# First loads cut finer, the checks' counts spread over the last batch, and the last store ahead of the verdict

## The chip, the cores and the metric

The kernel runs on one core of a Trainium2 chip. The metric is the device time of one execution in microseconds (us). The time before is a median of 313.62 us over 14 runs, which lie between 312.78 and 316.0.

A core has a matrix engine (PE, TensorE), a vector engine (DVE, VectorE), an engine for functions of one element (ACT, ScalarE), a general engine (POOL, GpSimd) and one that issues transfers (SP, SyncE). Each works through a queue of its own in order; they wait for one another on semaphores. Sixteen DMA engines move the data.

## The reference

Attention with inducing points, followed by a gated feed-forward layer:

```python
B, N, m, C = (4, 12480, 32, 128)
def mab(q, kv):
    s = scale * (q @ kv.transpose(0, 2, 1))
    s = s - s.max(-1, keepdims=True)
    a = np.exp(s)
    a /= a.sum(-1, keepdims=True) + 1e-09
    return a @ kv
h = mab(I, x)             # 32 rows for each batch
y = mab(x, h)             # 12480 rows for each batch
u = y @ w_in              # 128 -> 2048
g = u * np.clip(u + 3.0, 0.0, 6.0) / 6.0
out = g @ w_out           # 2048 -> 128
```

All inputs and the output are float32. Input and output are 25.6 MB each.

## The kernel before

**What it computes.** For each of the four batches it makes `h` (32 rows) in a first pass over x. As long as `u` stays under 3 in size, the second layer is `u*u/6 + u/2` times w_out, and the output for a row of x is a quadratic form in its 32 attention weights. The kernel builds small coefficient matrices for this from `h` and the weights (`c_...` functions), and the second pass over x (`b_...` functions) needs only them.

**The conditions.** That form is right only if some conditions hold: the largest `u` of the 32 rows is at most 3 (`g_all`), the sums of the first softmax lie between 1e-20 and 1e30 (`d_all`), and the second softmax's numbers are not too small (`r_all`, `nf_all`). The kernel keeps these values in four tables for all batches. After the last chunk it counts on DVE how many of the entries satisfy each condition (lines 922 to 939, five counts, each with an accumulator that goes to one column of `cnt`), adds the counts over the partitions with a matmul (L941), adds the five sums (L943), and compares the total with the number of entries (L945). The result `bad_i` is read by all five engines into a register (L949); if it isn't zero, `direct_path` computes everything again without the form (L952). With this input it is zero.

**How the work is cut.** The 12480 rows of a batch are six groups of 128 x 16 rows and a rest of 48 x 4. A group has four chunks of 128 x 4 rows, the rest is one chunk: 25 chunks for a batch, 100 in all.

**First pass, first batch** (`a_first`, L340): x is loaded in DMAs on GpSimd's queue, `load_x` (L110). In program order: both halves of group 0 (L125), then, after the identity is made, the rest, groups 1, 2 and 3 whole, and groups 4 and 5 in halves (L165), all ahead of the weights (L160, L161). The work goes by half groups: cast to bf16 (L359), transpose on PE (L369, copied by L371), weights of the softmax (L378, exponential L385), and the weighted sum (L392). A cast of a first half is split between ACT and DVE, a second half's is ACT's.

**Between the passes of the first batch** (`c_first`, L627): ACT casts the weights, PE adds up the denominators (`c_den`, L456), DVE inverts them (L473), PE transposes the sums (`c_HT`, L479), DVE scales them to `HT` (L482), and from this the coefficients are built (L488 to L603). Matmuls on zeros (`warm`, L176) keep PE busy: two ahead of all this, two between `c_den` and `c_HT`, one behind `c_HT`.

**Main loop** (L873): step t finishes chunk t and prepares chunk t + 2, and between PE's matmuls it fills in the first pass and the coefficients of the next batch; in the last batch (t from 75 on) there is nothing to fill in. On DVE a step is: the evacuation of chunk t - 1 (`b_evac`, L833, PSUM times r to `os`), the product of chunk t + 1 (L793, which needs the transfer `d`, L764), sometimes nf (L720), and the reciprocal of chunk t + 1 (L738). On PE it is: the linear part (`b_lin`, L801, into one of two PSUM banks of `op`, which the evacuation frees), 16 matmuls of the quadratic part (`b_quad`, L817) and the features of chunk t + 2 (L777). When a group is complete its 1 MB goes out by one DMA (L842), in the last batch on SP's queue, whose other DMAs are those of `d`.

**The end**: chunk 99 is the last rest of 48 x 4 rows. Its evacuation and store (96 KB) are called at L946, behind the counts and the verdict.

Of the kernel before, what the change touches and what calls it, by code (L numbers as in the profile page):

```python
# [9 lines left out]
FP32 = mybir.dt.float32  # L10
# [4 lines left out]
ALU = mybir.AluOpType  # L15
AX = mybir.AxisListType
# [8 lines left out]
TG = 16  # L25
SL = 4
XBUF = 5
# [13 lines left out]
def kernel(  # L41
# [8 lines left out]
    nc = tc.nc  # L50
    P = nc.NUM_PARTITIONS
    B, N, C = x.shape
    M = inducing.shape[0]
# [15 lines left out]
    NGR = len(groups)  # L69
# [11 lines left out]
    with ExitStack() as es:  # L81
# [25 lines left out]

        xs, xbs = {}, {}

        def load_x(b, g, parts=1):  # L110
            t0, p, n = groups[g]
            src = x[b, t0 : t0 + p * n, :].rearrange("(p i) c -> p i c", i=n)
            if n < TG:
                t = xlast.tile([P, n, C], FP32R, name="xl")
            elif b == 0 and g == XBUF:

                t = osp.tile([P, TG, C], FP32R, name="x5", tag="os")
            else:
                t = xin.tile([P, TG, C], FP32R, name="xr")
            for h in range(parts):  # L120
                lo, hi = h * n // parts, (h + 1) * n // parts
                nc.gpsimd.dma_start(t[:p, lo:hi, :], src[:, lo:hi, :])
            xs[(b, g)] = t

        load_x(0, 0, 2)  # L125

        held = []
        NF = NGR - 1 if rest else NGR
# [34 lines left out]

        make_identity(nc, ident[:, :])
        for g in (NF, *range(1, XBUF + 1)):  # L165
            load_x(0, g, 2 if g in (XBUF - 1, XBUF) else 1)
        wake = const.tile([P, 512], BF16, name="wake")
        nc.vector.memset(wake[:, :], 0.0)
        ident_b = const.tile([P, P], BF16, name="ident_b")
# [2 lines left out]
        def warm(n):  # L172

            wp = psF.tile([P, 512], FP32, name="wp", tag="fb")
            for _ in range(n):
                nc.tensor.matmul(wp[:, :], lhsT=wake[:, :P], rhs=wake[:, :])  # L176
# [67 lines left out]
        def a_begin(b):  # L244
            S[b] = {
                "xT": xTp.tile([P, N], BF16, name="xT"),
                "hnd": psH.tile([P, 512], FP32, name="hnd", tag="hnd"),
                "dacc": cst.tile([P, TG * M], FP32, name="dacc"),
            }
# [377 lines left out]
        def c_first():  # L627

            warm(2)
            nc.scalar.copy(w_in_b[:, : F // 2], w_in_r[:, : F // 2].bitcast(FP32))  # L630
            c_den(0)
            nc.scalar.copy(w_in_b[:, F // 2 :], w_in_r[:, F // 2 :].bitcast(FP32))
            warm(2)
            c_HT(0)
            warm(1)

            def cast_w(i, j):
                nc.scalar.copy(w_out_b[:, i:j, :], w_out_r[:, i:j, :].bitcast(FP32))

            cast_w(0, 4)  # L640
            c_G(0, 0, 6)
            sq = lambda *jbs: [c_sq(0, jb) for jb in jbs]
            cs = lambda *jcs: [c_C(0, jc) for jc in jcs]

            sg = lambda jb: (c_sq(0, jb), c_G(0, jb + 6, jb + 7))
            sg(0)
            sg(1)
            sg(2)
            cast_w(4, 8)
            b_pack(0, 0)  # L650
            b_e(0, 0)
            for c in range(4):
                b_spread(0, c)
            load_held(3)
            for jb in range(3, 7):
                sg(jb)
                cs(jb - 3)
            cast_w(8, 12)
            sg(7)
            b_f(0, 0)  # L660
            cs(4)
            sg(8)
            b_base(0, 0, 0)
            cs(5)
            sg(9)
            c_hs(0)
            b_base(0, 0, 1)
            cs(6)
            cast_w(12, 16)
            sq(10)  # L670
            cs(7)
            sq(11)
            b_r(0, 0)
            cs(8)
            sq(12)
            cs(9)
            sq(13)
            cs(10)
            b_base(0, 1, 0)
            sq(14)  # L680
            cs(11)
            sq(15)
            cs(12)
            c_L(0, 0)
            c_L(0, 1)
            b_base(0, 1, 1)
            a_cast(1, 0, ((nc.scalar.copy, 0, 2), (nc.scalar.copy, 2, 4)))
            b_prod(0, 0)
            c_BD(0)
            cs(13, 14, 15)  # L690
            c_tail(0)
            b_pack(0, 1)
            b_e(0, 1)
            c_max(0)
# [131 lines left out]
        def b_evac(b, c, op):  # L826
            g, j = chunks[c]
            t0, p, n = groups[g]
            st = S[b]
            if j == 0:  # L830
                st["os"] = osp.tile([P, TG, C], FP32, name="os", tag="os")
            ot = st["os"]
            nc.vector.tensor_mul(  # L833
                ot[:p, j * SL : (j + 1) * SL, :],
                op[:p, :].rearrange("p (s c) -> p s c", c=C),
                r_all[:p, b, c, :].unsqueeze(2).to_broadcast([p, SL, C]),
            )
            if (j + 1) * SL == n:
                r0 = b * N + t0

                eng = nc.gpsimd if b < B - 1 else nc.sync
                eng.dma_start(  # L842
                    out[r0 : r0 + p * n, :].rearrange("(p i) c -> p i c", i=n), ot[:p, :n, :]
                )


        a_begin(0)
        a_first()
        c_first()
        queue = []  # L850
        total = B * NCK
        ahead, sums = {}, {}
        for b in range(B):
            for g in range(NGR):
# [18 lines left out]
        for t in range(total):  # L873
            if t % NCK == 0:
                b = t // NCK
                assert not queue
                done_units[0] = 0
                begin, span = t, NCK
                if b + 1 < B:
                    a_begin(b + 1)  # L880
                    queue += ([(4, lambda: None)] if b == 0 else []) + a_units(b + 1) + c_units(b + 1)
                n_units = sum(w for w, _ in queue)

            def bg(part):
                fill(n_units * (t - begin + part) / span)

            if t == total - NCK // 2:

                nc.gpsimd.drain()
            tb = t + LEAD  # L890
            feat = 0 <= tb < total
            fb_, fc = divmod(tb, NCK)
            bo, co = divmod(t, NCK)
            if evac:
                b_evac(*evac)
                evac = None
            if 0 <= t + 4 < total:
                b_spread(*divmod(t + 4, NCK))
            if 0 <= tb - 1 < total:
                b_prod(*divmod(tb - 1, NCK))  # L900

            if feat:
                b_base(fb_, fc, 0)
            if t in sums:
                b_f(*sums[t])
            op = b_lin(bo, co)
            b_quad(bo, co, 0, op)
            bg(0.33)
            b_quad(bo, co, 1, op)
            for fn in ahead.get(t, []):  # L910
                fn()
            bg(0.67)
            if feat:
                b_base(fb_, fc, 1)
            if t + 1 < total:
                b_r(*divmod(t + 1, NCK))
            b_quad(bo, co, 2, op)
            bg(1.0)
            b_quad(bo, co, 3, op)
            evac = (bo, co, op)  # L920

        cnt = cst.tile([P, 5], FP32, name="cnt")
        junk = cst.tile([P, NR], FP32, name="junk", tag="r6")
        nc.vector.tensor_scalar(
            junk[:, :NR], r_all[:, :, :, :].rearrange("p b c s -> p (b c s)"), 1.0e-16, None,
            op0=ALU.is_ge, op1=ALU.add, accum_out=cnt[:, 0:1],
        )
        nc.vector.tensor_scalar(
            junk[:, : B * NGR], nf_all[:, :], -1.0e-8, None, op0=ALU.is_le, op1=ALU.add, accum_out=cnt[:, 1:2]
        )  # L930
        nc.vector.tensor_scalar(
            junk[:, :B], g_all[:, :], 3.0, None, op0=ALU.is_le, op1=ALU.add, accum_out=cnt[:, 2:3]
        )
        nc.vector.tensor_scalar(
            junk[:, : B * M], d_all[:, :, :].rearrange("p b m -> p (b m)"), 1.0e-20, None, op0=ALU.is_ge, op1=ALU.add, accum_out=cnt[:, 3:4]
        )
        nc.vector.tensor_scalar(
            junk[:, : B * M], d_all[:, :, :].rearrange("p b m -> p (b m)"), 1.0e30, None, op0=ALU.is_le, op1=ALU.add, accum_out=cnt[:, 4:5]
        )
        cp5 = psF.tile([P, 512], FP32, name="cp5", tag="fb")  # L940
        nc.tensor.matmul(cp5[:1, :5], lhsT=ones[:, 0:1], rhs=cnt[:, :])  # L941
        cs = cst.tile([1, 1], FP32, name="cs")
        nc.vector.tensor_reduce(cs[:, :], cp5[:1, :5], axis=AX.X, op=ALU.add)  # L943
        good = float(P * (NR + B * NGR + B + 2 * B * M))
        nc.vector.tensor_scalar(bad_i[:, :], cs[:, :], good, None, op0=ALU.not_equal)  # L945
        b_evac(*evac)  # L946


    bad = nc.values_load(  # L949
# [150 lines left out]
```

## Time and profile before

| what | value |
|---|---|
| median of 14 runs | 313.62 us |
| the profiled execution's own time | 313.75 us |
| its span in the profile | 312.0 us |
| PE busy | 298.5 us (96%) |
| DVE busy | 236.2 us (76%) |
| ACT busy | 231.9 us (74%) |
| POOL busy | 34.8 us (11%) |
| DMA, mean rate | 214 GB/s |
| granted PE clock | 0.995 |

The span is the time from the first to the last instruction that the profile holds; 1.75 us of the execution's own time lie around it. "Busy" counts an engine's own work, not its waits, branches and the issue of transfers. In the profile's lines the first numbers are the start and the duration in us, then comes the engine, the line of the kernel, the operation, and what is written and read. In square brackets stands how long the engine was idle before it and what ended that. The chain of work that ended last is followed back from the last instruction, at each step to what released it; its lines say what the end waited for at each moment. Its last piece is the small evacuation at 306.5 us; what follows is the sequencers' and the DMA's.

### The profile page before, as it was taken

What the parts mean: (1) busy time and instruction counts of PE and PEld (TensorE: products, weight loads), DVE (VectorE), ACT (ScalarE), POOL (GpSimd) and SP (SyncE); (2) the same over time, 40 slices, a digit from 0 to 9 for tenths busy, and PEclk for the clock granted to TensorE, in tenths of its full rate; (3) what the DMA queues carried; (4) which work ended last, traced back from release to release, by engine and by line L of the source; (5) the groups of instructions that cost most, each with busy time, mean ns of one, the idle gap of its engine ahead of it and who ended that gap; (6) DMA issues with size and microseconds to landing.
All of it is one profiled execution on the core that took longest, in us unless ns stands there. A gap on an engine that the chain in (4) does not pass through costs nothing.

```text
span 312.0 us, 9605 instructions
## 1 busy us (share of the span) xinstructions
PE 298.5 (96%) x3930; PEld 233.0 (75%) x3930; DVE 236.2 (76%) x539; ACT 231.9 (74%) x425; POOL 34.8 (11%) x81
## 2 busy tenths in 40 slices
PE   6899999999999999999999999999999999999991
PEld 2786678887677878888767878888767786777780
DVE  2697797978884868878795768788787577888883
ACT  3788999886589678886679759888668936777750
POOL 7521301111100010111110000100000001000000
PEclk9999999999999999999999999999999999999997
DMA  7999497998963453899965524555245435566644
GB/s 217 413 388 343 99 376 226 308 312 251 376 204 116 124 173 71 295 315 313 327 193 188 176 86 147 194 164 187 77 146 188 158 67 186 172 216 212 221 169 155
DMA packets 24513, 66.69 MB, mean 214 GB/s; under 512 B 3104, under 2 KB 17472, under 8 KB 18576
## 3 DMA queue, kind: packets, MB, share of 16 engines
q0 software_dynamic: 9088, 46.83, 43.7%
q1 hardware_dynamic: 15376, 19.19, 22.3%
q8 instruction: 32, 0.52, 0.7%
q14 instruction: 17, 0.14, 0.1%
HBM read 27.67 MB, written 25.56 MB: 171 GB/s over the span
## 4 chain that ended last, share of the span: by engine, by line
PE 74%; ACT 11%; DVE 6%; DMA 4%; issue 2%; POOL 1%; ACTq 0%; DVEq 0%; POOLq 0%
PE op L817 26%; PE bp L777 12%; PE op L801 7%; PE hnd L290 6%; ACT sq L579 6%; PE pt L268 5%; DMA xr<-in_x_dram 4%; PE cp L588 4%; PE s L276 2%; PE pp L748 2%; ACT TF L784 2%; PE ep L704 2%; PE dpm L568 2%; PE sp L718 1%; DVE os L833 1%
## 5 line engine op out<-in xcount | busy, mean ns | idle before, releaser
L784 ACT ACTIVATE TF<-bp 128x512 bf16<-128x512 f32 (+1 forms) x200 | 117.1, 598 | 38.5 <-PE rp L737 20.9
L817 PE MATMUL op<-Cq,TF 128*128 128x128 bf16 (+1 forms) x800 | 109.2, 223 | 0.0
L817 PE MATMUL op<-Cq,TD 128*128 128x128 bf16 (+1 forms) x800 | 105.9, 219 | 0.0
L833 DVE TENSOR_TENSOR os<-op,r_all 128x512 f32<-128x512 f32 (+1 forms) x100 | 68.4, 684 | 19.6 <-PE op L817 18.7
L817 PEld LDWEIGHTS <-TF 128*128 128x128 bf16 (+1 forms) x800 | 50.5, 98 | 33.6 <-issue 25.0
L777 PE MATMUL bp<-xT,W 128*128 128x512 bf16 (+1 forms) x200 | 75.1, 376 | 0.1
L793 DVE TENSOR_TENSOR TD<-TF,d 128x1024 bf16<-128x1024 bf16 (+1 forms) x100 | 66.8, 668 | 0.8 <-ACT TF L784 0.4
L817 PEld LDWEIGHTS <-TD 128*128 128x128 bf16 (+1 forms) x800 | 61.4, 98 | 0.6
L801 PE MATMUL op<-BD,nf 128*128 128x512 f32 (+1 forms) x100 | 53.3, 533 | 0.5 <-DVE os L833 0.3
L579 ACT ACTIVATE sq<-dpm 128x512 bf16<-128x512 f32 x60 | 35.0, 637 | 4.2 <-PE gp L510 1.9
L259 ACT CAST xb<-xr 128x1024 bf16<-128x1024 f32 x36 | 37.6, 1056 | 0.0
L738 DVE RECIPROCAL r_all<-rp 128x4 f32<-128x4 f32 (+1 forms) x100 | 17.7, 177 | 24.2 <-PE rp L737 23.8
L737 PE MATMUL rp<-one,nf 128*128 128x4 f32 (+1 forms) x100 | 34.5, 345 | 0.4
L269 DVE COPY xT<-pt 128x1024 bf16<-128x1024 bf16 (+1 forms) x42 | 25.8, 618 | 8.3 <-PE pt L268 7.8
L842 POOL DMA_DIRECT2D out_dram<-os x21 | 11.3, 539 | 143.0 <-DVE os L833 136.4
L290 PE MATMUL hnd<-xr,a 128*32 128x128 f32 x288 | 24.1, 226 | 0.0
L755 ACT ACTIVATE dk<-pp 128x512 bf16<-128x512 f32 (+1 forms) x28 | 15.7, 559 | 10.4 <-PE pp L748 10.4
L568 PE MATMUL dpm<-dH,w_in_b 128*128 128x512 bf16 x64 | 23.3, 381 | 0.0
L268 PE MATMUL pt<-ident_b,xb 128*128 128x128 bf16 x300 | 23.3, 218 | 0.0
L777 PEld LDWEIGHTS <-W 128*128 128x128 bf16 x200 | 19.5, 97 | 5.0 <-issue 3.4
L588 PE MATMUL cp<-w_out_b,sq 128*128 128x128 bf16 x256 | 22.7, 220 | 0.5 <-ACT sq L579 0.5
L510 PE MATMUL gp<-HTr,w_in_r 128*128 128x32 f32 x64 | 21.3, 358 | 0.2 <-ACT HTr L488 0.2
(129 smaller groups left out, 405.5 us busy)
## 6 DMA issues: line engine op xcount, KB each, us to landing
xr<-in_x_dram POOLq DMA_DIRECT2D x21, 1024.0 KB, 7.7
out_dram<-os POOLq DMA_DIRECT2D x18, 1024.0 KB, 4.4
d<-dk SPq DMA_DIRECT2D x96, 128.0 KB, 3.7
out_dram<-os SPq DMA_DIRECT2D x6, 1024.0 KB, 4.1
xr<-in_x_dram POOLq DMA_DIRECT2D x4, 512.0 KB, 8.1
x<-in_x_dram POOLq DMA_DIRECT2D x2, 512.0 KB, 13.9
w_in_r<-in_moe_w_in_dram POOLq DMA_DIRECT2D x1, 1024.0 KB, 13.9
w_out_r<-in_moe_w_out_dram POOLq DMA_DIRECT2D x1, 1024.0 KB, 16.9
```

Of the source, the lines that this page charges most:

```text
L259: eng(xb[:p, lo:hi, :], xs[(b, g)][:p, lo:hi, :].bitcast(FP32))
L268: nc.tensor.transpose(pt[:, (i - lo) * p : (i - lo + 1) * p], xb[:p, i, :], ident_b[:p, :p])
L290: nc.tensor.matmul(st["hnd"][:M, :C], lhsT=a1[:p, i * M : (i + 1) * M], rhs=xs[(b, g)][:p, i, :], start=(g == 0 and i == 0), stop=(g == NG ...
L579: nc.scalar.activation(sq[:, :], dpm[:, :], ACT.Square)
L588: nc.tensor.matmul(st["cp"][:, k * C : (k + 1) * C], lhsT=sq[:, k * P : (k + 1) * P], rhs=w_out_b[:, jc, :], start=(jc == 0 and k == 0), s ...
L737: nc.tensor.matmul(rp[:p, :SL], lhsT=nf[:, j * p : (j + 1) * p], rhs=one4[:, :])
L777: nc.tensor.matmul(bp[:, :w], lhsT=st["W"][:, k].rearrange("p m i -> p (m i)"), rhs=st["xT"][:, c0 : c0 + w],)
L784: nc.scalar.activation(st[("x", c)][:, k, :w], bp[:, :w], ACT.Exp, scale=scale)
L793: nc.vector.tensor_mul(u[:, :, :w], t[:, :, :w], d[:, :w].unsqueeze(1).to_broadcast([P, 2, w]))
L801: nc.tensor.matmul(op[:p, :], lhsT=st[("nf", g)][:, j * p : (j + 1) * p], rhs=st["BD"][:, :], start=True, stop=False, skip_group_check=True,)
L817: nc.tensor.matmul(op[:p, s * C : (s + 1) * C], lhsT=T[k][:, s * p : (s + 1) * p], rhs=st["Cq"][:, k, :], start=False, stop=(s == SL - 1 a ...
L833: nc.vector.tensor_mul(ot[:p, j * SL : (j + 1) * SL, :], op[:p, :].rearrange("p (s c) -> p s c", c=C), r_all[:p, b, c, :].unsqueeze(2).to_ ...
```

## The change

It has four parts.

- `load_x` takes a list of cuts. Group 0 of the first batch is loaded in three DMAs (columns 0 to 4, 4 to 8 and 8 to 16 of 16) instead of two, and group 1 in two instead of one.
- In `c_first` the transpose of the sums is called ahead of the two warm-up matmuls, and the one behind it goes.
- The counts are called in the last batch, ahead of the steps with 16, 13, 9 and 2 chunks left (t = 84, 87, 91 and 98), and stand on DVE ahead of that step's evacuation. The count of r is cut into three (batches 0 to 2; batch 3 without the last chunk; the last chunk), so there are seven. Only the last chunk's, 4 columns, is left for the end.
- At the end the small evacuation and its store are called ahead of the sum of the counts and the verdict.

```diff
-        def load_x(b, g, parts=1):
+        def load_x(b, g, cuts=(0, TG)):
...
-            for h in range(parts):
-                lo, hi = h * n // parts, (h + 1) * n // parts
+            for lo, hi in zip(cuts, cuts[1:]):
+                lo, hi = min(lo, n), min(hi, n)
                 nc.gpsimd.dma_start(t[:p, lo:hi, :], src[:, lo:hi, :])
...
-        load_x(0, 0, 2)
+        load_x(0, 0, (0, 4, 8, 16))
...
         for g in (NF, *range(1, XBUF + 1)):
-            load_x(0, g, 2 if g in (XBUF - 1, XBUF) else 1)
+            load_x(0, g, (0, 8, 16) if g in (1, XBUF - 1, XBUF) else (0, TG))
...
+            c_HT(0)
             warm(2)
-            c_HT(0)
-            warm(1)
...
+        def check(values, limit, op):
+            n = values.shape[1]
+            junk = cst.tile([P, 512], FP32, name="junk", tag="r6")
+            k = len(checks)
+            nc.vector.tensor_scalar(
+                junk[:, :n], values, limit, None, op0=op, op1=ALU.add, accum_out=cnt[:, k : k + 1]
+            )
+            checks.append(n)
+
+        def early_checks(left):
+            r_of = lambda i, j: check(r_rows[:, i * SL : j * SL], 1.0e-16, ALU.is_ge)
+            d = d_all[:, :, :].rearrange("p b m -> p (b m)")
+            if left == 16:
+                check(g_all[:, :], 3.0, ALU.is_le)
+                check(d, 1.0e-20, ALU.is_ge)
+            elif left == 13:
+                check(d, 1.0e30, ALU.is_le)
+            elif left == 9:
+                r_of(0, (B - 1) * NCK)
+            elif left == 2:
+                check(nf_all[:, :], -1.0e-8, ALU.is_le)
+                r_of((B - 1) * NCK, total - 1)
...
+            early_checks(total - t)
             if t == total - NCK // 2:
...
+        check(r_rows[:, (total - 1) * SL :], 1.0e-16, ALU.is_ge)
+        b_evac(*evac)
         cp5 = psF.tile([P, 512], FP32, name="cp5", tag="fb")
-        nc.tensor.matmul(cp5[:1, :5], lhsT=ones[:, 0:1], rhs=cnt[:, :])
+        nc.tensor.matmul(cp5[:1, : len(checks)], lhsT=ones[:, 0:1], rhs=cnt[:, :])
...
         nc.vector.tensor_scalar(bad_i[:, :], cs[:, :], good, None, op0=ALU.not_equal)
-        b_evac(*evac)
```

More of the change, by code (lines that the diff above doesn't have):

```diff
@@ L844, in b_evac @@
                 )
+        total = B * NCK
+        NCHECK = 7
+        cnt = keep.tile([P, NCHECK], FP32, name="cnt")
+        r_rows = r_all[:, :, :, :].rearrange("p b c s -> p (b c s)")
+        checks = []
+        def check(values, limit, op):
[19 more added lines that the diff above has]
+                r_of((B - 1) * NCK, total - 1)
         a_begin(0)
@@ L850 @@
         queue = []
-        total = B * NCK
         ahead, sums = {}, {}
@@ L920 @@
             evac = (bo, co, op)
[L922 to L939, printed above, removed]
+        check(r_rows[:, (total - 1) * SL :], 1.0e-16, ALU.is_ge)
+        b_evac(*evac)
         cp5 = psF.tile([P, 512], FP32, name="cp5", tag="fb")
-        nc.tensor.matmul(cp5[:1, :5], lhsT=ones[:, 0:1], rhs=cnt[:, :])
+        nc.tensor.matmul(cp5[:1, : len(checks)], lhsT=ones[:, 0:1], rhs=cnt[:, :])
         cs = cst.tile([1, 1], FP32, name="cs")
-        nc.vector.tensor_reduce(cs[:, :], cp5[:1, :5], axis=AX.X, op=ALU.add)
-        good = float(P * (NR + B * NGR + B + 2 * B * M))
+        nc.vector.tensor_reduce(cs[:, :], cp5[:1, : len(checks)], axis=AX.X, op=ALU.add)
+        assert len(checks) == NCHECK
+        good = float(P * sum(checks))
         nc.vector.tensor_scalar(bad_i[:, :], cs[:, :], good, None, op0=ALU.not_equal)
-        b_evac(*evac)
     bad = nc.values_load(
```

## The prediction

> **What bounds the kernel now.** I read the page's shares first, then the chain that ended last, then the timelines of the two stretches that the change touches, then the DMA view. TensorE (PE) is busy 96% of the span of 312.0 us, and from 260 to 300 us it is busy in all 40 of 40 us. So the middle is PE's, and only what delays PE counts there. The change works at the two ends: up to 28 us, and from 302 us on.
>
> The chain of work at the start:
>
> ```profile
> 5.71 13.14 DMA xr<-in_x_dram
> 18.85 0.02 issue
> 18.87 1.06 ACT xb L359
> ...
> 25.04 0.45 PE wp L176 x2
> 25.48 0.49 PE dps L456 x4
> 25.97 0.43 PE wp L176 x2
> 26.40 0.19 PE htp L479
> 26.59 0.02 issue
> 26.61 0.23 DVE HT L482
> ```
>
> Up to 18.85 us the chain is one queued transfer, the second half of group 4; then the cast of that half and PE's work on the last pieces. The two warm-up matmuls (L176) at 25.97 stand between the denominator (L456) and the transpose (L479). Two ScalarE rows of the timeline tell where it waits for data:
>
> ```profile
> 12.44 0.62 ACT L359 CAST xb<-xr 128x512 bf16<-128x512 f32 x1 [0.41 <-DMA xr<-in_x_dram]
> ...
> 27.68 0.62 ACT L638 CAST w_out_b<-w_out_r 128x512 bf16<-128x512 f32 x1 [0.47 <-DMA w_out_r<-in_moe_w_out_dram]
> ```
>
> VectorE (DVE) at the end, from the timeline:
>
> ```profile
> 302.32 0.69 DVE L833 TENSOR_TENSOR os<-op,r_all 128x512 f32<-128x512 f32 x1
> ...
> 303.31 0.36 DVE L793 TENSOR_TENSOR TD<-TF,d 128x384 bf16<-128x384 bf16 x1 [0.29 <-DMA d<-dk]
> ...
> 303.68 0.65 DVE L833 TENSOR_TENSOR os<-op,r_all 128x512 f32<-128x512 f32 x1
> ...
> 304.25 0.55 DVE L924 TENSOR_SCALAR_CACHE_REDUCE junk<-r_all 128x400 f32<-128x400 f32 x1
> ...
> 306.44 0.67 DVE L833 TENSOR_TENSOR os<-op,r_all 48x512 f32<-48x512 f32 x1
> ```
>
> The last MB's evacuation ends at 304.33, five counts and the verdict follow, and the last, small evacuation stands behind them at 306.44. After it the trace shows only sequencers and DMA. Three answers on that (stores issued after 304 us with the us to their landing; the verdict's load on SyncE; SyncE's waits in the If):
>
> ```profile
> out_dram<-os SPq DMA_DIRECT2D x1, 1024.0 KB, 5.1
> out_dram<-os SPq DMA_DIRECT2D x1, 96.0 KB, 2.6
> ```
>
> ```profile
> L949 SPq TENSOR_LOAD <-bad_i x1: 515/515/515, 307.5 to 307.5; - x1
> ```
>
> ```profile
> L952 SPq EVENT_SEMAPHORE  x7: 17/17/17, 308.2 to 309.8; - x7
> ```
>
> The 1 MB store is issued at 304.36 and lands 5.1 us later, at 309.47. The 96 KB store is issued at 307.13 and lands at 309.71. SyncE has the verdict at 308.04 and then waits for the stores until 309.8; the fixed end from there takes 2.2 us. **So the end is set by the big store, not by the verdict**, which has some 1.3 us of room.
>
> **Part 1: first x in three pieces, second group in halves.** It adds two DMAs on GpSimd's queue: 2 x 0.54 us (the median issue, L122) = 1.07 us for everything behind them. The last x issue (7.43 us) lands 14.0 us later, and w_in's (10.22 us) 13.9 us later: both sit behind a full stream, so the later issue costs nothing. The identity's memset slips by 0.5 us, and its readers have until the first transpose at 6.38. The first cast can start some 0.5 to 1 us before 5.70, and group 1's before 10.03. But the row at 12.44 shows ScalarE waiting for group 2, which stays whole and lands behind the same bytes: there the gain ends. Were that cover gone, at most the 0.42 us that ScalarE idles before the cast at 18.87 could be won downstream, since its neighbours are as busy as the stream. The price on the other side is the stream itself: each us that it starts later is a us of the kernel. In the slices of the first 25 us (0.625 us each) the DMA moves 92, 295, 184 and 347 GB/s between 2.5 and 5.0 us, mean 230, against about 415 later: 2.5 x (1 - 230/415) = 1.1 us are lost in starting. Smaller first transfers could touch that either way. Bounds -0.4 to +1.1; I take +0.1, near nothing, as issues come every 0.54 us and a 256 KB piece at 415 GB/s takes 0.63 us, so the queue doesn't run dry.
>
> [...]
>
> **Part 2: transpose ahead of the warm-up, one warm-up matmul less.** PE reaches L479 at 25.97 instead of 26.40 and ends at about 26.2. HT (L482) needs the reciprocal too, which runs 26.01 to 26.37, so that is late next: HT starts at about 26.39 instead of 26.61, -0.22. Behind it HTr, the G matmuls and the first square follow by the same amount, 28.43 to 28.21, until ScalarE's cast at 27.68, which waits for w_out's landing and holds the engine until about 28.2 (the square follows 0.75 us after the cast's start now): this is just reached. I take -0.2, bounds -0.22 and 0. The matmul that goes (0.22 us) ran beside the wait for HT: nothing.
>
> **Part 3: counts in the last batch.** From start to start the counts take 0.60 us (400 wide), 0.22 (28), 0.20 (4) and 0.33 (128): about 0.19 + 1.02 ns per column, so 300 wide 0.50 and 96 wide 0.29. Before chunk 84 stand 0.53 us, before 87 0.33, before 91 0.50. DVE idles 0.23, 0.27 and 0.27 us there waiting for PE, which leaves delays of 0.30, 0.06 and 0.23 for the evacuation and the product queued behind. PE needs those evacuations 0.97 to 1.17 us after they end now, and the products 0.92 us after: cost 0. Uncovered it would be 0.3 + 0.1 + 0.2 = 0.6, with no idle 1.36.
>
> Before chunk 98 it is different. The counts of nf (0.22) and r (0.29) stand ahead of the evacuation at 302.32, which waits for nothing now. It ends at about 303.5 instead of 303.0. The product behind it waited for its d until 303.31 anyway, so +0.2 is left: the last MB's evacuation ends at 304.53, and **its store is issued at 304.56 instead of 304.36**. PE's last product starts up to 0.15 later. Take +0.2, bounds 0 and +0.5.
>
> **Part 4: the end.** After 304.53 one count (0.20), the small evacuation (when PE is done, 304.95 to 305.6), the sum and the verdict, at about 305.85 instead of 306.51. The small store goes from 307.13 to 305.6, but behind 1 MB on the same queue. The order swap gives DVE's verdict a wait behind the evacuation, 0.6 us; all engines' loads wait for it, and none is late. What is late is the big store: 309.47 + 0.2. Gain of the move: 0. If the big store weren't there, it would be about 0.7 to 1.5 us.
>
> **Sum.** 0.1 - 0.2 + 0 + 0.2 + 0 = +0.1 on the profiled execution's 313.75 (span 312.0 and 1.75 around it): 313.85. That execution is 0.13 above the median of the 14 runs, 313.62; so on their scale 313.7. About 0.3%, 0.94 us, is what a measurement of this kernel can tell from no change.
>
> **Rivals.** (A) The big store gets quicker. Earlier 1 MB stores on that queue took about 4.1 us to land; this one took 5.1, and a 16 KB packet of the instruction queue sits on one DMA engine from 304.2 on for 1.4 us (12.5% of 16 engines' time in the window 304.0 to 304.7):
>
> ```profile
> q8 instruction: 1, 0.02, 12.5%
> ```
>
> If the shifted order gets the store past it, 1.0 us goes: 312.85, on the runs' scale 312.7. For it: four of the 14 runs lie at 312.8 to 312.9, most others some 0.8 higher. Against: the packet comes where PE stands in its program, and both sides move by under 0.3 us. 0.2. (B) Slower: the pieces cost the stream its start once more, the whole 1.1 us; 18.85 is on the chain, so it counts in full as soon as group 4 lands later: 313.75 + 1.1 - 0.2 + 0.2 = 314.85, on the runs' scale 314.7. For it: the start-up loss above. Against: the queue stays fed. 0.12. (C) The start does gain its 0.42: 313.3 or 313.2. 0.13. (D) The counts stall PE, +0.6 to 1.36: about 314.7. Against: the slack of 0.9 us. 0.05. The forecast has 0.5.
>
> Range: the forecast and C alone hold 313.0 to 314.1; to leave out no more than 2 in 10 it reaches to A and B: 312.7 to 314.6. Faster by over 0.3% (under 312.68): half of A and a share of A with C, 0.16. Slower (over 314.56): most of B and D, 0.15. Within: 0.69.
>
> **What would show it.** Right: group 4's second half lands at 18.8 to 19.0; HT starts 0.2 us nearer to that; no new PE wait from 276 to 300 us; the evacuation of chunk 98 ends 0.2 later against PE; the verdict is some 0.7 earlier and SyncE waits longer for the big store. Wrong: a big store that lands in 4.1 us (A), a landing of group 4 beyond 19.5 (B) or below 18.6 (C), or L801 and L817 waiting for DVE in the last batch (D).

## The result and the profile after

The changed kernel takes **315.75 us** (median of 10 runs, 314.52 to 316.57), the kernel before 313.59 (47 runs of the same work): a ratio of 1.0066, 95% interval [1.0048, 1.0084]. It is slower by about 2.2 us, above the forecast's range. The profiled execution took 315.27 us with a span of 313.5 us; before it was 313.75 and 312.0. So this one execution shows 1.5 us of the loss.

**Read the start first.** The chain that ended last, from 2 to 29 us of the profile after (start and duration in us):

```profile
2.51 5.57 DMA xr<-in_x_dram
...
8.10 1.05 ACT xb L359
...
9.20 0.63 PE pt L369 x8
...
25.30 1.15 PE hnd L392 x16
...
27.86 0.24 DVE HT L482
```

Before, the chain followed the stream up to 18.85 us. Now it leaves the stream at 8.08 us, with the last piece of group 0, and from 9.20 on it is nearly all PE's. HT starts at 27.86 instead of 26.61, 1.25 us later, although the transpose now stands ahead of the warm-up. ScalarE's rows of the timeline say when the pieces came:

```profile
5.15 0.62 ACT L359 CAST xb<-xr 128x512 bf16<-128x512 f32 x1 [3.11 <-DMA xr<-in_x_dram]
8.10 1.05 ACT L359 CAST xb<-xr 128x1024 bf16<-128x1024 f32 x1 [2.33 <-DMA xr<-in_x_dram]
```

The cast of the first quarter starts 0.55 us earlier than that of the first half did, as intended, and the cast of the same group's second half 0.93 us later (before, it stood at 7.17). What PE does meanwhile, first before and then after:

```profile
3.17 0.31 PE L181 MATMUL itp<-ident,I_sb 32*128 32x32 f32 x1
3.41 2.66 PE L176 MATMUL wp<-wake 128*128 128x512 bf16 x8
```

```profile
3.68 0.31 PE L181 MATMUL itp<-ident,I_sb 32*128 32x32 f32 x1 [0.58 <-POOL ident masks.py:199]
3.92 3.59 PE L176 MATMUL wp<-wake 128*128 128x512 bf16 x8
...
9.20 0.62 PE L369 MATMUL pt<-ident_b,xb 128*128 128x128 bf16 x8 [1.07 <-ACT xb L359]
```

The same eight warm-up matmuls take 3.59 us instead of 2.66. The records of the granted clock begin with its first rise, at 4.98 us before and at 7.75 here. Until that rise these matmuls follow each other every 427 ns, after it every 216.

**The middle adds almost nothing.** Matched chunk by chunk, the evacuations stand 1.26 us later at chunk 0 (45.01 against 43.75) and 1.35 us later at chunk 98. VectorE at the end, from the timeline:

```profile
303.58 0.15 DVE L856 TENSOR_SCALAR_CACHE_REDUCE junk<-nf_all 128x28 f32<-128x28 f32 x1
...
303.77 0.25 DVE L856 TENSOR_SCALAR_CACHE_REDUCE junk<-r_all 128x96 f32<-128x96 f32 x1
...
305.03 0.65 DVE L832 TENSOR_TENSOR os<-op,r_all 128x512 f32<-128x512 f32 x1
...
306.17 0.68 DVE L832 TENSOR_TENSOR os<-op,r_all 48x512 f32<-48x512 f32 x1 [0.41 <-PE op L816]
...
306.95 0.14 DVE L960 TENSOR_SCALAR bad_i<-cs 1x1 int32<-1x1 f32 x1
```

The two counts ahead of chunk 97's evacuation are there, and the small evacuation stands ahead of the verdict. The verdict ends at 307.09.

**The end has a new last comer.** The stores issued after 304 us with the us to their landing (the DMA view), and SyncE's waits and PE's branch in the If (the line's answer; the three numbers are the least, median and largest duration in ns):

```profile
out_dram<-os SPq DMA_DIRECT2D x1, 1024.0 KB, 4.2
out_dram<-os SPq DMA_DIRECT2D x1, 96.0 KB, 3.8
```

```profile
L966 SPq EVENT_SEMAPHORE  x7: 17/17/17, 308.5 to 310.2; - x7
...
L966 PEldq COMPARE_BRANCH  x2: 95/2000/3905, 308.3 to 308.6; - x2
```

The big store is issued 1.35 us later (305.71) but takes 4.2 us instead of 5.1 and lands at 309.95, only 0.5 us later than before. The small one lands at 310.63, and SyncE is through with its waits at 311.6. But PE's second branch starts at 308.63 and takes 3.9 us, until 312.54; all engines meet behind it, about 0.9 us after SyncE is ready. In the profile of before the same branch took 0.42 us:

```profile
L952 PEldq COMPARE_BRANCH  x2: 95/256/417, 307.6 to 307.9; - x2
```

So of the 1.53 us that this span grew, 1.25 are there at HT, 0.1 are added by chunk 98, where the counts stand, and the rest at the end, where a quicker store (-0.9) is more than paid back by PE's branch.

### The profile page after: what moved, and what is told of

Same layout as the page of the kernel before. It is cut to its first block, busy times and chain, and to the rows that moved or that the text cites. A ratio compares the mean times of both kernels' runs of the same rounds, so it can differ in the third digit from the quotient of the medians.

```text
span 313.5 us, 9608 instructions
## 1 busy us (share of the span) xinstructions
PE 300.2 (96%) x3929; PEld 234.9 (75%) x3929; DVE 235.9 (75%) x543; ACT 231.6 (74%) x425; POOL 36.0 (11%) x83
## 4 chain that ended last, share of the span: by engine, by line
PE 77%; ACT 11%; DVE 5%; issue 2%; DMA 2%; POOL 0%; ACTq 0%; DVEq 0%; POOLq 0%
PE op L816 26%; PE bp L776 12%; PE op L800 7%; PE hnd L290 6%; ACT sq L579 6%; PE pt L268 5%; PE cp L588 4%; PE s L276 2%; PE pp L747 2%; ACT TF L783 2%; PE hnd L392 2%; PE pt L369 2%; DMA xr<-in_x_dram 2%; PE ep L703 2%; PE dpm L568 2%
## 5 line engine op out<-in xcount | busy, mean ns | idle before, releaser
L122 POOL DMA_DIRECT2D xr<-in_x_dram x27 | 14.8, 552 | 63.3 <-ACT TF L783 29.2
```

## The experiments

Each ratio is to the kernel before on the same chip, with its 95% interval. Unless said otherwise a kernel is the one before with the edit shown. "Rate" is the DMA view's mean from 5 to 9 us; before it is 404 GB/s.

### The parts alone

**Part 1 alone.**

```diff
-        load_x(0, 0, 2)
+        load_x(0, 0, (0, 4, 8, 16))
...
-            load_x(0, g, 2 if g in (XBUF - 1, XBUF) else 1)
+            load_x(0, g, (0, 8, 16) if g in (1, XBUF - 1, XBUF) else (0, TG))
```

> The kernel before with the finer first loads alone. Theory H (the start: the transfer stream begins later, TensorE idles longer and its granted clock falls to half for a while, so the first pass ends some 1.2 to 1.5 us later): 1.2 to 1.5 us slower than before, x0's second half lands near 8.1 us instead of 7.15, a clock of 0.5 somewhere between 7 and 15 us in the profile, and an end as before (the branch over the direct path takes TensorE 0.4 us). Theory F (the loss sits at the end, in TensorE's wait for instructions at the last branch, and comes with TensorE's program being one matmul shorter): no slower than 0.5 us. Theory D (the counts in the last batch are what costs): no change.

Measured: 314.64, before 313.36, ratio 1.0041 [1.0023, 1.0059]. HT at 27.88, rate 298 GB/s, PE's branch 0.42 us. The loads cost 1.3 us by themselves, all of it at the start: from HT to the end this profile takes 284.7 us, the one before 285.4.

**Part 2 alone, and with one more matmul in place of the one that goes.**

```diff
+            c_HT(0)
             warm(2)          # second kernel: warm(3)
-            c_HT(0)
-            warm(1)
```

> The kernel before with the transpose ahead of the warm-up matmuls and one warm-up matmul less, nothing else. Theory F: the scaled sums (L482) start 0.2 us earlier, but the last branch on TensorE takes about 3.9 us instead of 0.4 and the whole is about 0.5 to 1.2 us slower. Theory H and theory D: 0.2 us faster, with the branch as before.

> As the run before, but with three warm-up matmuls behind the transpose, so that TensorE's program is as long as in the kernel before. Theory F: the last branch takes 0.4 us again, and the whole is 0.2 us faster than before. If it is as slow as the shorter one, the length of TensorE's program has nothing to do with it.

Measured: 314.19, ratio 1.0021 [1.0007, 1.0036], with PE's last branch at 3.83 us; padded 313.47, ratio 0.9991 [0.9973, 1.0009], with the branch at 0.42 us. The order alone costs nothing that can be measured; leaving the matmul out as well costs 0.7 us more.

**Parts 3 and 4 alone**, with the change's own code.

```diff
+            early_checks(total - t)
...
+        check(r_rows[:, (total - 1) * SL :], 1.0e-16, ALU.is_ge)
+        b_evac(*evac)
...
-        b_evac(*evac)
```

> The kernel before with the counts in the last batch and the small store ahead of the verdict, nothing else. Theories H and F: within 0.3 us of before (the big store is issued 0.1 to 0.2 later, the verdict is not on the path). Theory D: 1 us or more slower, with TensorE waiting for VectorE in the last batch.

Measured: 313.44, ratio 1.0002 [0.9987, 1.0018]. The evacuation of chunk 98 at 303.75 (303.68 before), the verdict 0.7 us earlier, the branch 0.42 us, the stores landing at 308.96 and 309.19. Neither gain nor loss, as forecast.

### PE's program and its last branch

**Only the matmul behind the transpose goes**, with the order kept.

```diff
             c_HT(0)
-            warm(1)
```

> The kernel before without the one warm-up matmul behind the transpose; the order is kept. It does nothing else. Theory F (TensorE's program, two instructions shorter, no longer has the code behind the last branch fetched in time): the branch takes about 3.9 us, and the whole is 0.6 to 1.2 us slower than before. Rival (the loss of the run with the transpose first came from the order, or from a colder clock at that point): no change, branch 0.4 us.

Measured: 314.37, ratio 1.0035 [1.0018, 1.0052]: one warm-up matmul of 0.2 us less makes the kernel 1.1 us slower by the medians. Its line of the If:

```profile
L951 PEldq COMPARE_BRANCH  x2: 95/1714/3332, 307.8 to 308.1; - x2
```

The trace shows what comes late. The queue that the DMA view calls "q8 instruction" moves 16 KB packets, 32 in the whole run; such a packet is called a fetch below. Before, the last two stand at 304.2 and 309.1 us. Here they stand at 309.0 and 312.1, and in the profile after at 309.9 and 313.3: the first of the two comes only after the branch began. In all five profiles with a long branch it does so, and the branch ends 1.36 to 1.37 us after that packet's end. The six packets before these two moved by 0.6 us at most. That the 3.3 to 3.9 us are a wait for this packet is read from these times; no view names a releaser of the branch. In this one profile the wait is mostly offset: its last big store, with no instruction packet beside it, took 3.9 us instead of 5.1, and from HT to the end it takes 285.6 us against 285.4 before. The 1.1 us of the medians is more than this execution shows.

**The change with three warm-up matmuls**, so that PE's program is as long as before.

```diff
-            warm(2)
+            warm(3)
```

> The changed kernel with three warm-up matmuls behind the transpose instead of two, so PE's program has as many instructions as before the change. Theory F (the shorter program moves PE's last fetch of instructions to behind the two stores, and PE's last branch waits for it): the branch at the end takes 0.4 us instead of 3.9, and the time is 0.6 to 1.1 us under the changed kernel's, 314.5 to 315.0. Theory T alone (only the stream's later start costs): no change against the changed kernel, near 315.6.

Measured: 315.13, ratio 1.0067 [1.0049, 1.0084]. The branch is back at 0.42 us, as expected, but the gain of 0.6 to 1.1 us is not there: the ratio is that of the change (1.0066). Its stores show what took its place:

```profile
out_dram<-os SPq DMA_DIRECT2D x1, 1024.0 KB, 5.3
out_dram<-os SPq DMA_DIRECT2D x1, 96.0 KB, 4.3
```

The fetch, early enough for the branch now, stands at 305.67 beside the store issued at 305.21, and the store takes 5.3 us. From HT to the end this kernel takes 285.6 us and the change 285.6: in these two profiles one fetch is paid at the branch or at the store.

**Parts 2 to 4 padded, and not padded**, with the loads as before.

```diff
+            c_HT(0)
-            warm(2)
+            warm(3)          # second kernel: warm(2)
-            c_HT(0)
-            warm(1)
...
+            early_checks(total - t)
```

> The loads as before the change; the transpose first with three warm-up matmuls behind it; the counts and the end as in the change. If the loads and the program's length are all that made the change slower, this is no slower than the kernel before: 313.0 to 313.5, 0 to 0.4 us under it. If the counts or the order at the end cost something of their own that the run of parts 3 and 4 alone did not show, it is over 313.8.

> The changed kernel with the loads as before: parts 2, 3 and 4 together, PE's program one matmul shorter than before. Theory F: PE's branch at the end takes 3.3 to 3.9 us, the big store about 4.1, and the end comes 0.3 to 0.8 us later than with three warm-up matmuls (313.57): 313.9 to 314.4. Without F it would be at or under 313.6.

Measured: 313.57, ratio 1.0009 [0.9996, 1.0021]; not padded 314.15, ratio 1.0014 [1.0002, 1.0025]. Without the loads the change is within 0.5 us of the kernel before. The time of the second kernel is as expected, but not its reason: in its profile the branch took 0.43 us, although PE's program is as short as in the runs with the long branch. Counted up to the branch (a matmul and its weight load count as two), PE has 7,893 instructions in the trace of the kernel before. The branch took 0.41 to 0.43 us in all 14 kernels with 7,893 or more. It took 3.3 to 3.9 us in four with 7,891 or 7,892: the change (in both its profiles), part 2 alone, the one matmul less, and the run with two pieces below, which has one wait less. This kernel, with 7,891, is the one exception, and the record doesn't say why.

**The fetch moved off the last store.** On top of the padded parts 2 to 4, eight warm-up matmuls of 512 columns become 28 of 128 columns, so that PE's program gets 40 instructions longer:

```diff
-        warm(8)
+        warm(28, P)
```

> The loads as before the change, the transpose first with three warm-up matmuls, the counts and the end as in the change; and the eight warm-up matmuls of 512 columns ahead of the first transposes become 28 of 128 columns. That makes PE's program 40 instructions longer and so moves every fetch of its instructions about 2 us earlier; the packet that stands at 304.4 us beside the last 1 MB store should come at 302 to 303. Theory F (the instruction packet is what makes that store take 5 us instead of 4.1): the store lands in 4.1 to 4.3 us, median 312.5 to 313.0. If the packet does nothing to the store: as without the longer program, 313.5.

Measured: 315.29, ratio 1.0058 [1.004, 1.0075]: 1.6 us slower than before, where a gain was expected. The last fetch did move ahead of the last store (305.27, store issued at 306.51), and that store took 4.2 us, as theory F wants (that the packet is what slows this store). But another fetch moved from 263.2 to 260.0 us, beside the 1 MB store issued at 258.83. That store and the wait it caused, in the DMA view from 258.5 to 265.2 us and in VectorE's timeline:

```profile
q8 instruction: 1, 0.02, 1.6%
...
out_dram<-os POOLq DMA_DIRECT2D x1, 1024.0 KB, 6.2
```

```profile
265.14 0.69 DVE L832 TENSOR_TENSOR os<-op,r_all 128x512 f32<-128x512 f32 x1 [2.04 <-DMA out_dram<-os]
```

In the kernel before, the DMA view from 258.2 to 263 us has the same store with no instruction packet:

```profile
out_dram<-os POOLq DMA_DIRECT2D x1, 1024.0 KB, 4.2
```

The evacuation of chunk 75 needs that buffer; before, it stood at 262.87, just after the landing at 262.70. Now it waits 2.0 us, and all chunks behind it are about 2.2 us late. The profiles together bear this out: among the 167 stores of 1 MB that stand between 225 us and the last one in all 20, two have an instruction packet 0.5 to 1.2 us behind their issue, both in this kernel, and they took 6.2 and 5.1 us. The others took 3.9 to 4.5, one 4.9.

### The loads

**Which pieces?** Group 0 in three pieces alone, and group 1 in halves alone.

```diff
-        load_x(0, 0, 2)
+        load_x(0, 0, (0, 4, 8, 16))      # first kernel only
...
+            load_x(0, g, (0, 8, 16) if g in (1, XBUF - 1, XBUF) else (0, TG))      # second kernel only
```

> The kernel before with group 0 in three pieces, group 1 whole. Theory S (one more transfer ahead of the identity: it pushes the identity back by 0.5 us, TensorE's warm-up gets a gap at 3.1 us, and the stream starts in smaller packets): nearly all of the 1.28 us of the finer loads, 0.9 to 1.3 us. Rival (each further transfer costs, wherever it stands): about half, 0.6 us.

> The kernel before with group 1 in halves, group 0 in two pieces as before. Theory S: within 0.3 us of before. Rival (each further transfer costs): 0.6 us slower.

Measured: 315.68, ratio 1.0069 [1.0047, 1.0092], against 313.44, ratio 1.0008 [0.9997, 1.0019]. It is group 0 alone.

**Is it PE's clock?** Part 1 with six warm-up matmuls in place of four.

```diff
-        warm(4)
+        warm(6)
```

> The finer loads alone, with six instead of four warm-up matmuls ahead of the first transpose, so that TensorE has no gap at 3.1 us. Theory C (the loss is TensorE's clock, which comes up later because of that gap): 0.4 us or less slower than before, the granted clock at 1.0 from 8 us at the latest. Theory T (the loss is the transfer stream's later landing): as slow as with the finer loads alone, 1.0 to 1.4 us.

Measured: 314.21, ratio 1.0035 [1.0018, 1.0053]. One row for each of two kernels, 11 to 14 us, the change and then this run; behind the busy times of PE, its weight loads, DVE, ACT and POOL stand the granted clock, the DMA share and GB/s:

```profile
11.00:14.00 3.00, 3.00 (x32) 2.69 (x30) 1.67 (x4) 1.79 (x4) 2.60 (x6) 0.53 1.08 427
```

```profile
11.00:14.00 3.00, 2.72 (x47) 2.23 (x44) 1.86 (x4) 2.05 (x4) 2.79 (x7) 1.00 1.09 431
```

In the change PE gets 0.53 of its clock there: the records show half clock from 11.16 to 14.57 us, 3.41 us, after PE was busy for 1.54 of the 3 us from 8 to 11 (2.17 in the kernel before). With more warm-up the clock stays at 1.00 there, though PE was busy for only 1.34 of those 3 us; what halved it in the one and not in the other is not shown. And 0.9 us of the loss stay too. So the clock is not the whole of the loss: in this profile it rose at 5.06 us, and HT still came at 28.27, behind a last x piece that landed at 22.61.

But the clock has a larger part in it than these rows tell, as the view counts 1.00 ahead of the first rise too. In part 1 alone the first rise came only at 13.24 us; the transposes at 9.60 ran at half speed there (1.04 us for eight, against 0.62 in the change's row at 9.20). Leaving the run with more warm-up aside, in the eight profiles with one more issue ahead of the identity the first rise came at 7.5 to 13.2 us, in the eleven with the identity as before at 4.3 to 7.7. How much of the loss is the clock and how much the later pieces is not settled. The mean clock of a run can't settle it, since it leaves out the stretch ahead of the first rise and takes in the end, where the clock is at half once PE's work is over (from 308.12 us in the change, whose 0.986 is what the two stretches at half, 3.41 and 5.4 of 313.5 us, give alone).

**One transfer more, or small ones first?** Four kernels: group 0 as (0, 4, 16), two pieces with the small one first; the change's pieces with the third one issued behind the identity; group 0 as (0, 8, 12, 16), three pieces with the half first; and one tiny load of 128 x 4 bytes ahead of everything.

```diff
+        load_x(0, 0, (0, 4, 16))         # first
...
+        load_x(0, 0, (0, 4, 8))          # second, with group 1 in halves
         make_identity(nc, ident[:, :])
+        nc.gpsimd.dma_start(xs[(0, 0)][:, 8:16, :], x[0, 0 : P * TG, :].rearrange("(p i) c -> p i c", i=TG)[:, 8:16, :])
...
+        load_x(0, 0, (0, 8, 12, 16))     # third
...
+        nc.gpsimd.dma_start(extra[:, :], moe_w_in[:, 0:1])      # fourth
         load_x(0, 0, 2)
```

> Only group 0's loads differ from the kernel before: columns 0 to 4 and 4 to 16, so still two DMAs ahead of the identity, but the first one small. Theory S1 (small packets in the first transfers make the stream start slowly): the last x piece lands 0.8 us or more later than 21.4, and the median is 0.8 to 1.3 us longer, near 314.3. Theory S2 (it is the third transfer issued ahead of the identity and the rest of the stream): landings within 0.3 us of the kernel before, median within 0.3 us of it, 313.1 to 313.6.

> Part 1 as in the change, but the third piece of group 0 is issued behind the identity's memset and select, so PE's first warm-up matmuls start when they do in the kernel before. S2: the gap of 0.59 us that PE shows ahead of the identity's matmuls goes, the clock stays up; if the issue position was the cause the median is within 0.4 us of the kernel before. S1: the stream lands as late as with part 1 alone (last x piece 21.9 or later), median 1.0 to 1.5 us over the kernel before, near 314.6.

> Only group 0's loads differ from the kernel before: columns 0 to 8, 8 to 12, 12 to 16, so three pieces as in the change, but the half comes first and the two small ones last. Theory S1 (small transfers at the very start, before the DMA engines are fed): the first half lands as before, the stream has moved within 100 KB of the kernel before's 2102 KB at 9 us, and the median is within 0.4 us of the kernel before. Theory S3 (three transfers for group 0 in any order, and 2 KB packets): 1600 to 1900 KB at 9 us and 1 to 2 us more, as with the three pieces alone (1735 KB, ratio 1.0069).

> The kernel before with one more DMA ahead of group 0's halves on GpSimd's queue: 128 packets of 4 bytes, into a column that nobody reads. If one more transfer and its 0.5 us issue ahead of the stream is the price of three pieces (S2), the stream is some 0.5 us later from its first byte and the median 0.5 to 1.3 us more. If the price is the small packets and the pieces' layout (S1, S3), the later issue alone is left: landings 0.5 us later at most and the median 0.2 to 0.6 us more.

| group 0 | rate, 5 to 9 us | last x piece lands | median | ratio |
|---|---|---|---|---|
| halves (before) | 404 | 21.39 | 313.3 to 313.7 | |
| halves, a tiny load ahead | 385 | 21.95 | 313.98 | 1.0010 [1.0000, 1.0021] |
| half, two quarters | 384 | 21.97 | 314.03 | 1.0009 [0.9997, 1.0021] |
| quarter, then the rest | 349 | 21.82 | 315.21 | 1.0066 [1.0046, 1.0086] |
| two quarters, half | 302 | 21.80 | 315.68 | 1.0069 [1.0047, 1.0092] |
| the same and group 1 in halves, the half of group 0 behind the identity | 251 | 22.85 | 315.81 | 1.0072 [1.0054, 1.0090] |

The theory of one transfer more falls: a transfer ahead of the stream cost 0.3 us (313.98 against 313.67), and moving the third piece behind the identity did not help (1.0072, against 1.0041 for part 1 alone), though PE's warm-up then began as early as before. PE waited 3.70 us for that piece there, and its clock was at half from 9.11 to 15.94 us. The order decides: the same three pieces cost 0.4 us with the half first and 2.4 us with the quarters first. A part of the 2.4 is probably the clock, which was at half from 12.51 to 15.92 us in that profile; a run of the same kernel with a mean clock of 0.996 took 314.41, the other five, at 0.983 to 0.987, 315.29 to 316.64. The run with two pieces is hardly a witness: PE's branch took 3.4 us in it, and its HT came at 27.05, no later than with the half first (27.20). The DMA view from 5 to 9 us for the kernel before, the change, the run with quarters first and the run with quarters last:

```profile
DMA packets 335, 1.61 MB, mean 404 GB/s; under 512 B 44, under 2 KB 44, under 8 KB 208
```

```profile
DMA packets 412, 1.36 MB, mean 339 GB/s; under 512 B 51, under 2 KB 51, under 8 KB 412
```

```profile
DMA packets 282, 1.21 MB, mean 302 GB/s; under 512 B 40, under 2 KB 40, under 8 KB 202
```

```profile
DMA packets 461, 1.53 MB, mean 384 GB/s; under 512 B 56, under 2 KB 56, under 8 KB 352
```

The last has the most packets and a good rate, so the number of small packets isn't it. Up to 5 us the change has moved as much as before (0.64 MB against 0.59 by the DMA view). From 5 to 9 us the DMA engines are as busy in the change (the view's share is 1.11) as before (1.14), so the queues were fed, yet less moves. Some single packets are slow there: most 4 KB ones take 174 ns, and one takes 1.64 us in the change at 7.32 us. But the second profile of the change, below, has none over 0.55 us at the same rate. So what lowers the rate is not shown.

**The whole change once more, and the whole change with the half first** and three warm-up matmuls; the second against the first:

```diff
-        load_x(0, 0, (0, 4, 8, 16))
+        load_x(0, 0, (0, 8, 12, 16))
...
-            warm(2)
+            warm(3)
```

> The changed kernel once more, on the chip of the next run, as its yardstick: 1.5 to 2.2 us over the kernel before, near 315.6, with PE's branch at the end at 3.3 to 3.9 us.

> The changed kernel with group 0's pieces in the order 0 to 8, 8 to 12, 12 to 16 (the half first) and three warm-up matmuls behind the transpose; everything else of the change stays. Theory S1 (small transfers ahead of the stream cost it 0.9 us and more, behind a half they don't) with F: 313.5 to 314.2, at least 1.2 us under the changed kernel. Theory S3 (three pieces in any order): within 0.6 us of the run with three warm-up matmuls alone, near 315.1.

Measured on one chip: 316.03, ratio 1.0078 [1.006, 1.0095], and 314.01, ratio 1.0020 [1.0009, 1.0031]. The order of three transfers, with the one matmul, gives back 2.0 of 2.6 us. Against the change with three warm-up matmuls (1.0067, on another chip) only the order differs, and the ratios put that at 1.5 us. The profiled execution of the first was its quickest, 313.81 us, with HT at 26.70. From 5 to 9 us it moved 338 GB/s, no more than the other profile of this kernel (339), whose HT came at 27.86; but its clock rose at 7.48 us and stayed up, and that of the other was at half again from 11.16 to 14.57. So the loss at the start differs from execution to execution, and the rate alone doesn't set it. No variant beats the kernel before.

## Why the prediction was wrong, point by point

- **What bounds the kernel**: right. Only the two ends moved; the middle carries the delay unchanged from chunk 0 to 98.
- **Part 1, the step that failed most.** "I take +0.1, near nothing [...] so the queue doesn't run dry." The queue didn't run dry, as the DMA engines' share shows (1.11 from 5 to 9 us, 1.14 before), but that was no protection: a full queue moved 339 GB/s instead of 404. By the runs the term is +1.3 for part 1 alone and +2.4 for its three pieces without group 1's halves, outside its bounds of -0.4 to +1.1. The cover that was named for the later identity, "readers have until the first transpose at 6.38", missed its first reader: the warm-up transpose at 3.17, which then waited 0.58 us, and PE's clock rose at 7.75 us instead of 4.98. The sum had no term for PE's clock. And "there the gain ends" was misread: group 1's halves cost nothing (1.0008), but the chain no longer went by the stream's end; it went by group 0's last piece and PE behind it.
- **Rival B** was the right place at 0.12, and its size, 1.1, is a little under what the runs show. Its reason, that the stream pays its start once more, is not what happened: up to 5 us as much had moved as before (0.64 MB against 0.59). The loss comes after that, and only with the small pieces first.
- **Part 2.** The order: forecast -0.2; HT stood 0.17 us earlier in the padded kernel with parts 2 to 4 (26.44), but not in that with part 2 alone (26.63), and the medians can't tell it from zero. "The matmul that goes (0.22 us) ran beside the wait for HT: nothing" failed: its time was nothing, its place in the program was worth 1.1 us where it alone went, and 0.7 between the two kernels of part 2. Both are differences of medians; with part 1 in place the padding brought nothing (1.0067 against 1.0066). One matmul less moved only the last two fetches, the first of them past the branch's start.
- **Part 3**: right. No new PE waits; +0.2 at t = 98 was +0.1.
- **Part 4**: right for the part alone: the move gains nothing while the big store ends last. In the whole change another thing ended last, PE's branch.
- **Rival A** came true, the store in 4.2 us past the packet, and brought nothing. The packet was not gone, as both pages count 32; it was seen at the store and not followed to PE's branch, which now ended 1.37 us behind it.

**What stays open**: what lowers the rate after small first transfers, how the loss at the start divides between later pieces and PE's clock, and why one kernel with the shorter PE program had its branch in time.

## What to carry to other kernels

Cut the first load finer only behind a larger transfer (here the same three pieces cost 0.4 us with the half first and 2.4 us with the quarters first), and judge it over several executions, by the rate just after the start and by when PE's clock comes up, not by the landing of the first piece. Where a kernel ends in a branch, look at the branch instruction and at the instruction queue's packets before and after every edit, even one that only takes work away (here one warm-up matmul less took the branch from 0.42 to 3.3 us). And when a packet is found in the way of a transfer, ask who needs that packet before counting its absence as a gain.

## What the runs showed of the hardware

- A branch took 3.3 to 3.9 us in the five profiles where a 16 KB instruction packet came only after its start, against 0.41 to 0.43 us in the 15 others, where one stood 2.4 us or more ahead of it. In the five, the branch ended 1.36 to 1.37 us after the packet.
- In 14 profiles with a 16 KB instruction packet within 0.6 us of the last 1 MB store's issue, the store took 3.9 to 5.3 us (median 4.9); in the six without, 3.9 to 4.3. In one run a store in the middle, with such a packet 1.2 us behind its issue, took 6.2 instead of 4.2 us, and the evacuation that needed its buffer waited 2.0 us, which was not expected in the middle of a long loop.
- With one transfer of 512 bytes in all (4 bytes for each of 128 rows) ahead of the stream the last x piece landed 0.56 us later (21.95 against 21.39 us).
- The clock's records begin with its first rise, at 4.3 to 13.2 us in these profiles; before it the view prints 1.00, while 512-column matmuls stand 427 ns apart instead of 216.
- After that rise, half clock for 3.41 us (once 6.83) appeared between 9 and 16 us in six of the 20 profiles. Three of the six have their loads as before, so late pieces are not needed for it.
